# Down-weight sums dealt anew over the units of a GeGLU kernel, and raw down weights fetched a unit ahead

## The chip, the cores and the metric

The kernel runs on one core of a Trainium2 chip. The metric is the device time of one execution in microseconds (us). A core has five engines with queues of their own: TensorE (PE) for matmuls, VectorE (DVE), ScalarE (ACT), GpSimd (POOL) and SyncE (SP), which here issues all DMA transfers. SBUF is the on-chip memory, PSUM the eight banks into which TensorE writes, HBM the memory outside.

## The reference

```
def reference(x, w_gate, w_up, w_down):
    g = jnp.einsum("bsd,df->bsf", x, w_gate)
    u = jnp.einsum("bsd,df->bsf", x, w_up)
    h = _gelu(g) * u
    return jnp.einsum("bsf,fd->bsd", h, w_down)
```

x is 1 x 2048 x 1024, w_gate and w_up are 1024 x 3584, w_down is 3584 x 1024, all bf16. `_gelu` is the tanh form.

## The kernel before, in words

**Arithmetic.** Each of the three products is made by a Strassen-like scheme on 2 x 2 blocks: seven block products in place of eight, bought with sums of blocks. Sums of weights are called s1 to s4 (and sa, a cast), sums of x are t1 to t4 (and tb), and partial results that more than one output needs are taken out of PSUM by ACT (`snap`, L124) as p1, u2 and p5. Products of raw blocks run in bf16, products of sums in f32r. Two passes (`ip` = 0, 1) cover 1024 rows each, in two halves `c` of 512.

**Units.** The 3584 columns of gate and up are 14 units of 256. In pass 0, unit 0 is done plainly, units 1 to 3 and 12, 13 by `unit` (L239), units 4 to 11 two at a time by `pair0` (L339), which applies the scheme a second time to one product of the pair and saves two partial results, p5, to HBM (`pd`) for pass 1, where `pair1` (L437) reads them back. Each unit leaves two row blocks of h = gelu(g) * u; VectorE makes the product (`times`, L107 in the profile, as is every VectorE operation of this kind), ACT the gelu (L199). After its units, each pass runs `down` (L616), which multiplies h by w_down: first raw bf16 products that need `raw` slices of w_down (`fetch12`, L581: fourteen of 256 KB), then the forms with the sums ("w,q" in the profile).

**Sums of w_down.** w_down has 14 blocks `j`, and each needs three sums m. They are made once, in pass 0, stored to HBM (`td`) and read in both passes. Two ways exist. `keep_part` (L504) lets ACT copy a raw part into a free PSUM bank and VectorE subtract (three ACT and three DVE operations per block). `keep_whole` (L520) uses three POOL operations:

```
        m = [slot([P, N], f32r, "m") for _ in range(3)]
        pool(m[0], ra[:, N:], ra[:, :N], SUB)
        pool(m[1], rb[:, N:], m[0], SUB)
        pool(m[2], rb[:, :N], m[1], SUB)
```

`JS` (L62) deals the blocks to the pairs: the first two of an entry are made by ACT and DVE, a third by POOL. `making` (L783) deals the rest to units 12 and 13. `fetch_wd` (L491) loads the raw blocks they need, two transfers of 256 KB for each block.

**Order.** The order on SP, DVE and POOL, on PE, and mostly on ACT, is that of the program text (`manual_schedule`); each engine works strictly in that order and waits by semaphores. Memory is dealt by pools: `kpool` has 52 slots of 2 KB per partition, handed round in the order of the program (`slot`); a new tile takes a slot only when all that used the old one is done. So a change in the number of tiles moves every later tile to another slot, and with it the wait that comes before the tile's first write. `wpool` has three buffers of 8 KB (weights of a unit, some big loads, the staging `st8` for h), and other pools have one buffer for a name or tag.

**Memory for h.** `hT` holds the first 14 row blocks in SBUF. While `forms` (sums of x for the pairs) and `saved` (the partial results of a pair) are in use, there is no room for the rest, so units 7 to 11 write to `st8`, go out to HBM (`hd`, `keep_home` L336) and come back once `forms` and `saved` are free (five transfers out, five back, in `prepare` of unit 12, L880).

**Hooks.** `unit` calls `aside(0)` behind its first product, `keep` for the sums of w_down, and `prepare` as `after_p5`, where the next unit's sums are issued to POOL; `turned` (units 2 and 3) makes sums of x. `pair0` calls `hooks` with "w" (load a unit's weights), "made" (store m), "out", "pd" and "fetch". `more` (L939) puts the last stores of m into `down`, and `todo` runs an agenda of loads by step.

Of the kernel before, what the change touches and what calls it, by code (L numbers as in the profile page):

```python
# [10 lines left out]
def kernel(  # L11
# [23 lines left out]
    nc = tc.nc  # L35
# [23 lines left out]
    NWARM = 7  # L59
    SLOTS = 52  # L60
    FIRST, LAST = 4, 11
    JS = {4: (0, 1, None), 6: (2, 3, 4), 8: (5, 6, 7), 10: (8, 9, None)}  # L62
    JB = [js[1] for js in JS.values()]
    LAG = 3
    BIG12 = (0, 2, 4)
# [13 lines left out]
    def new_x():  # L79
        return [xpool.tile([P, NKB, N], bf16, name=f"xT{c}") for c in range(2)]  # L80

    NA = 10
    hT = hpool.tile([P, NJ, 2, N], bf16, name="hT")
    forms = hpool.tile([P, NA, N], f32r, name="forms", tag="h1")
    saved = hpool.tile([P, NJ - NA, N], f32, name="saved", tag="h2")
    h1 = {}

    def h1_part(n):
        if n not in h1:
            shape = [P, (NA, NJ - NA)[n], 2, N]  # L90
            h1[n] = hpool.tile(shape, bf16, name=f"hT{n}", tag=("h1", "h2")[n])
        return h1[n]

    def h(kh, j, c):
        at = hT if kh == 0 else h1_part(j >= NA)
        return at[:, j - NA * (kh and j >= NA), c, :]
    wdn = w_down.rearrange("(kh j p) d -> p kh j d", kh=2, p=P)

    def slot(shape, dtype, name):
# [139 lines left out]
    def unit(u, banks, s, t, late, after_p5, aside, keep, ahead_of_p4, behind_p4, turned):  # L239
        GU = range(2)  # L240
        e, c, d = banks
        aside(-2)
        g, up = late() if late else (None, None)
        aside(-1)
        for i in GU:
            product(e[i], s["s2"][i], t["t2"], False)
        aside(0)
        keep(0, c)
        u2 = [snap(e[i], "u2") for i in GU]
        if late:  # L250
            g = gelu(g)
        c11 = g, up
        keep(1, c)
        keep(2, c)
        c = d
        for i in GU:
            product(c[i], s["s1"][i], t["t1"], True)
        p5 = [snap(c[i], "p5") for i in GU]
        after_p5()
        for i in GU:  # L260
            product(e[i], s["s3"][i], t["t3"], False)
        if turned:
            g, up = add(e, p5)
            times(2 * u + 1, 1, gelu(g), up)
            turned(banks[1])
        else:
            g, up = new(dve, e[0], p5[0], ADD, "sum", dtype=f32), banks[1][not late]
            dve(up, e[1], p5[1], ADD)
        if late:
            times(2 * u, 0, *c11)  # L270
        for i in GU:
            product(c[i], s["s4"][i], t["tb"], False)
        if not turned:
            times(2 * u + 1, 1, gelu(g), up)
        aside(1)
        g, up = add(c, u2)
        times(2 * u, 1, gelu(g), up)
        ahead_of_p4()
        for i in GU:
            product(e[i], s["sa"][i], t["t4"], False)  # L280
        behind_p4()
        if turned:
            dve(e[1], e[1], p5[1], SUB)
        times(2 * u + 1, 0, gelu(e[0]), e[1])
# [1 line left out]

    H = KH // 2
    T1, T2, T3, T4, TB = [[forms[:, 2 * n + i] for i in range(2)] for n in range(5)]
    A, B = [[saved[:, 2 * n + i] for i in range(2)] for n in range(2)]
    pd = dpool.tile([P, LAST - FIRST + 1, 2, N], f32, name="pd")  # L290
    hd = dpool.tile([P, LAST - NU // 2 + 1, 2, 2, N], bf16, name="hd")
    lo = hT[:, 10:14].rearrange("p j c n -> p (j c) n")

    def small_sums(s, q):
# [39 lines left out]
        times(fb, c, g, up)  # L334

    def keep_home(u):  # L336
        nc.sync.dma_start(out=hd[:, u - NU // 2], in_=away[u][:, u % 2])

    def pair0(a, roles, S, t, js, hooks):  # L339
        F, C, K, E = roles  # L340
# [1 line left out]
        sa, sb = S[a], S[b]  # L342
        q = {}
        t1 = t["t1"]

        sa.make(*[x for x in ("s1", "s2", "s3") if x not in sa])
        sb.make(*[x for x in ("s1", "s2") if x not in sb])
# [11 lines left out]
            times(fb, 0, gelu(e[0]), e[1])  # L359

        def keep(j, n, ps):
            if j is not None:
                keep_part(j, n, ps[n % 2])

        ja, jb, jp = js
        if jp is not None:
            keep_whole(jp)
        hooks("w", n)
        keep(ja, 0, K)
        full(F, sa["s2"], t["t2"])  # L370
        u2a = [snap(F[i], "u2", spare[2 + i]) for i in range(2)]
        part(E, [x[:, :H] for x in sa["s1"]], t1[:H], True, False)
        p1 = [snap(E[i], "p1", A[i]) for i in range(2)]
        full(C, sb["s2"], t["t2"])
# [1 line left out]
        keep(ja, 2, K)  # L376
        hooks("made", ja)
        part(E, [x[:, H:] for x in sa["s1"]], t1[H:], False)
        p5a = [snap(E[i], "p5", spare[i]) for i in range(2)]
        u2b = [snap(C[i], "u2") for i in range(2)]  # L380
        full(F, sa["s3"], t["t3"])
        g, up = add(F, p5a)
# [1 line left out]
        full(E, sa["s4"], t["tb"])  # L384
        g = gelu(g)
        times(2 * a + 1, 1, g, up)
        hooks("made", jp)
        part(K, q["r2"], T2, False)
        u2r = [snap(K[i], "u2", B[i]) for i in range(2)]
        full(F, sa["sa"], t["t4"])  # L390
# [15 lines left out]
            dve(B[i], E[i], u2r[i], ADD)  # L406
        hooks("pd", a)
        hooks("fetch", a)
        p5b = [snap(K[i], "p5", spare[i]) for i in range(2)]
        raw1(F, W(n))  # L410
        g, up = add(C, p5b)
        p1n = [snap(F[i], "p1") for i in range(2)]
# [76 lines left out]
    wraw, made = {}, {}  # L489

    def fetch_wd(js):  # L491
        big = None
        for j in js:
            if j < NJ - 2:
                wraw[j] = [slot([P, Dm], bf16, "raw") for _ in range(2)]
            else:
                if big is None:
                    big = wpool.tile([P, 4, Dm], bf16, name="w")
                n = 2 * (j - NJ + 2)
                wraw[j] = [big[:, n + kh] for kh in range(2)]  # L500
            for kh in range(2):
                nc.sync.dma_start(out=wraw[j][kh], in_=wdn[:, kh, j, :])

# [15 lines left out]

    def keep_whole(j):  # L520
        ra, rb = wraw[j]
        m = [slot([P, N], f32r, "m") for _ in range(3)]
        pool(m[0], ra[:, N:], ra[:, :N], SUB)
        pool(m[1], rb[:, N:], m[0], SUB)
        pool(m[2], rb[:, :N], m[1], SUB)
        made[j] = m

    def store_made(j):
        if isinstance(made[j], list):
# [56 lines left out]

    agenda = {}

    def at(step, what, j):
        agenda.setdefault(int(step), []).append((what, j))

    for n in range(NJ):
        at(max(-1, 2 * n - 8), fetch12, n)
    for j in range(NJ):
        at(AT12[j], load12, j)
        at(AT12S[j], make12, j)
# [183 lines left out]

    def making(u):  # L783
        if u == NU - 2:
            return [10]
        return [11, 12, 13] if u == NU - 1 else []

    E, K, C, F = odd, cc, dd, even
    spare = [flat(xT[1][:, 2 * m : 2 * m + 2]) for m in range(4)]
    S, p5 = {}, {}  # L790

    def W(u):
# [39 lines left out]
    for ip in range(NPASS):  # L832
        with tc.manual_schedule(engines={ENG.Activation}):
# [6 lines left out]
            for u in range(1 if ip == 0 else 0, NU):  # L840
                if upgraded(u):
                    if u % 2:
                        continue
                    if u == FIRST:
                        S = {u: s, u + 1: sums_s(W(u + 1), pool)}
                        if ip == 0:
                            st8 = wpool.tile([P, 2, 2, 2, N], bf16, name="w")
                            away.update({n: st8 for n in range(NU // 2, LAST + 1)})

                    def hooks(what, n):  # L850
                        if what == "w":
                            W(n)
                            if ip and n <= LAST:
                                fetch_p5(n)
                        if what == "out" and n in away:
                            keep_home(n)
                        if what == "pd":
                            j = 0 if n % 2 else 2
                            nc.sync.dma_start(out=pd[:, n - FIRST], in_=saved[:, j : j + 2])
                        if what == "made" and n is not None:  # L860
                            store_made(n)
                        if what == "fetch":
                            js = JS.get(n + 2, making(LAST + 1))
                            fetch_wd([j for j in js if j is not None])

                    roles = F, C, K, E
                    if ip == 0:
                        F, C, K, E = pair0(u, roles, S, t, JS[u], hooks)
                    else:
                        F, C, K, E = pair1(u, roles, S, t, hooks)  # L870
                    if u + 1 == LAST:
                        s = make_s(None, pool, S[u + 2])
                        nxt["s"] = S[u + 3]
                        if ip == 0:
                            away.clear()
                    continue
# [3 lines left out]
                def prepare():  # L880
# [2 lines left out]
                    if u + 1 < NU:  # L883
                        nxt["s"] = make_s(W(u + 1), pool, nxt.get("s"))
                    if ip == 0:
                        if len(js) == 1:
                            store_made(js[0])
                        for j in js[1:]:
                            keep_whole(j)
                        if u >= LAST:  # L890
                            fetch_wd(making(u + 1))
                        if u == NU - 2:
                            for n in range(NU // 2, LAST + 1):
                                j = 2 * n - NJ
                                nc.sync.dma_start(out=h1_part(0)[:, j : j + 2], in_=hd[:, n - NU // 2])
                        if u == FIRST - 2:
                            fetch_wd(JS[FIRST][:2])

# [6 lines left out]
                def aside(part):  # L905
                    if first and part < 0:
                        rest_of_0(part + 2)
                    if part == 0 and u + 2 < NU:
# [2 lines left out]
                            fetch_p5(u + 2)  # L911
                        if (ip, u) == (0, 1):
                            load_lo()
                    if part == 0 and "t4" not in t:
                        t.make("t4")

# [73 lines left out]
```

## Time and profile before

| | |
|---|---|
| median of 3 runs | 549.48 us (549.23 to 550.05) |
| the profiled execution | 549.2 us |
| its span, first to last instruction | 547.4 us |
| mean granted TensorE clock | 0.997 |
| TensorE busy | 536.6 us, 2393 matmuls |
| DVE, ACT, POOL busy | 362.2, 276.4, 272.1 us |
| HBM read, written | 81.26 MB, 22.02 MB |

The span begins with the first and ends with the last instruction of the profiled execution; 1.8 us of its time lie around it. In the lists of groups and in the timeline, a row names the engine, the line, what is written and what is read ("bank<-raw,hT": into a PSUM bank, from `raw` and `hT`), the number of instructions, and in brackets the idle time ahead of the row and what ended it. Times in the timeline count from the start of the span. All matmuls have L131, POOL's sums L110, VectorE's operations L107, ACT's gelu L199, ACT's copies out of PSUM L124, ACT's casts of raw parts into PSUM L513. Pass 0 ends its units at about 201 us, and `down` of pass 0 begins at about 204 us.

### The profile page before, as it was taken

How to read it: one execution, taken by the hardware profiler on the slowest of the kernel's cores; microseconds unless marked ns; L12 is line 12 of the kernel's file. 1: busy time of each engine (PE TensorE's matmuls, PEld its weight loads, DVE VectorE, ACT ScalarE, POOL GpSimd, SP SyncE). 2: the span in 40 equal slices, each digit the busy share in tenths (PEclk: the TensorE clock that was granted, in tenths of full speed). 3: DMA queues.
4: the chain of work that ended last, by engine and by line, in shares of the span. 5: the costliest groups of instructions: out<-in, count | busy, mean ns of one | idle time of the engine just before them, and what ended most of it. 6: DMA issues, size and time to landing. Idle time of an engine off the chain costs nothing.

```text
span 547.4 us, 7631 instructions
## 1 busy us (share of the span) xinstructions
PE 536.6 (98%) x2393; PEld 377.6 (69%) x2393; DVE 362.2 (66%) x556; ACT 276.4 (50%) x497; POOL 272.1 (50%) x253
## 2 busy tenths in 40 slices
PE   9999999999999979999999999999999999999997
PEld 5568586757577654488886868667677685478885
DVE  2988867576776879258687464585765839766730
ACT  2557676777685740015543556556666561114431
POOL 1079937989898750000005966668988940000000
PEclk9999999999999999999999999999999999999999
DMA  9797046477779499999995643332642239673751
GB/s 242 176 230 198 1 135 219 164 265 247 249 260 325 158 363 399 375 305 204 231 290 172 174 116 117 111 112 85 193 126 69 76 113 385 214 229 98 222 190 50
DMA packets 119560, 107.99 MB, mean 197 GB/s; under 512 B 22240, under 2 KB 98016, under 8 KB 119520
## 3 DMA queue, kind: packets, MB, share of 16 engines
q1 hardware_dynamic: 119520, 107.50, 64.8%
q8 instruction: 19, 0.31, 0.2%
q14 instruction: 21, 0.17, 0.1%
HBM read 81.26 MB, written 22.02 MB: 189 GB/s over the span
## 4 chain that ended last, share of the span: by engine, by line
PE 77%; DMA 9%; POOL 5%; DVE 4%; issue 2%; ACT 2%; POOLq 0%; DVEq 0%; SPq 0%; ACTq 0%
PE bank L131 76%; DMA raw<-in_w_down_dram 7%; POOL s L110 3%; POOL r L110 2%; DMA pd<-saved 1%; DVE bank L107 1%; DMA td<-m 1%; ACT g L199 1%; PE bank L753 1%; DVE sum L107 1%; PE bank L698 1%; DVE m L107 1%; DVE hT L107 1%; ACT bank L513 0%; DVE w L107 0%
## 5 line engine op out<-in xcount | busy, mean ns | idle before, releaser
L110 POOL TENSOR_TENSOR s<-w 128x512 fp32r<-128x512 bf16 x102 | 122.1, 1217 | 143.3 <-PE bank L131 111.3
L131 PE MATMUL bank<-t,s 128*128 128x512 f32 x552 | 132.4, 392 | 0.6 <-DVE m L107 0.3
L131 PEld LDWEIGHTS bank<-t,s 128*128 128x128 f32 x552 | 103.3, 188 | 24.0 <-DVE m L107 0.8
L131 PE MATMUL bank<-xT,w 128*128 128x512 bf16 (+1 forms) x504 | 110.5, 376 | 0.4 <-ACT forms L824 0.4
L131 PEld LDWEIGHTS <-w 128*128 128x128 bf16 x504 | 47.7, 98 | 58.9 <-issue 4.9
L199 ACT ACTIVATE g<-sum 128x512 f32<-128x512 f32 x81 | 51.4, 634 | 70.2 <-DVE sum L107 64.6
L124 ACT COPY p<-bank 128x512 f32<-128x512 f32 x92 | 51.7, 589 | 43.3 <-PE bank L131 42.8
L110 POOL TENSOR_TENSOR s<-s,w 128x512 fp32r<-128x512 f32 x50 | 58.9, 1197 | 5.0 <-PE bank L131 4.7
L107 DVE TENSOR_TENSOR sum<-bank,p 128x512 f32<-128x512 f32 x54 | 36.4, 687 | 35.7 <-PE bank L131 35.7
L131 PE MATMUL bank<-q 128*128 128x512 f32 x240 | 58.9, 389 | 0.0
L110 POOL TENSOR_TENSOR s<-w,s 128x512 fp32r<-128x512 bf16 x50 | 57.6, 1176 | 0.0
L107 DVE TENSOR_TENSOR hT<-g,bank 128x512 bf16<-128x512 f32 x68 | 46.2, 688 | 16.5 <-ACT g L199 10.1
L131 PE MATMUL bank<-t,sa 128*128 128x512 f32 x216 | 55.1, 397 | 0.0
L131 PE MATMUL bank<-tb,s 128*128 128x512 f32 x216 | 54.8, 395 | 0.0
L131 PEld LDWEIGHTS bank<-q 128*128 128x128 f32 x240 | 45.1, 188 | 9.3
L119 ACT CAST tb<-raw 128x512 fp32r<-128x512 bf16 x28 | 17.3, 626 | 64.5 <-DMA raw<-in_w_down_dram 28.1
L131 PE MATMUL bank<-raw,hT 128*128 128x512 bf16 x192 | 43.6, 390 | 3.6 <-DMA raw<-in_w_down_dram 3.6
L131 PEld LDWEIGHTS bank<-tb,s 128*128 128x128 f32 x216 | 40.2, 188 | 9.9 <-POOL s L110 1.1
L131 PEld LDWEIGHTS bank<-t,sa 128*128 128x128 f32 x216 | 40.6, 188 | 9.1
L124 ACT COPY u<-bank 128x512 f32<-128x512 f32 x54 | 30.5, 594 | 17.8 <-PE bank L131 17.8
L131 PEld LDWEIGHTS <-hT 128*128 128x128 bf16 x192 | 19.2, 100 | 27.8 <-issue 6.7
L119 ACT CAST sa<-w 128x512 fp32r<-128x512 bf16 x54 | 30.9, 621 | 0.1
(81 smaller groups left out, 640.4 us busy)
## 6 DMA issues: line engine op xcount, KB each, us to landing
raw<-in_w_down_dram SPq DMA_DIRECT2D x76, 256.0 KB, 5.2
q<-td SPq DMA_DIRECT2D x60, 256.0 KB, 5.3
w<-in_w_gate_dram SPq DMA_DIRECT2D x27, 512.0 KB, 4.1
w<-in_w_up_dram SPq DMA_DIRECT2D x27, 512.0 KB, 5.4
td<-m SPq DMA_DIRECT2D x24, 256.0 KB, 3.8
w<-td SPq DMA_DIRECT2D x6, 1024.0 KB, 10.0
td<-m SPq DMA_DIRECT2D x6, 768.0 KB, 6.4
pd<-saved SPq DMA_DIRECT2D x8, 512.0 KB, 6.0
```

Of the source, the lines that this page charges most:

```text
L107: nc.vector.tensor_tensor(out=out, in0=a, in1=b, op=op)
L110: nc.gpsimd.tensor_tensor(out=out, in0=a, in1=b, op=op)
L119: nc.scalar.copy(out=t, in_=src)
L124: nc.scalar.copy(out=t, in_=ps)
L131: nc.tensor.matmul(ps, lhsT=lhs, rhs=rhs, start=start, stop=stop, skip_group_check=True)
L199: nc.scalar.activation(g, src, ACT.Gelu_apprx_tanh)
L698: nc.tensor.transpose(tp[:, ko, :], xn[i][:, ko * P : (ko + 1) * P], ident)
L753: nc.tensor.matmul(bank[3][:, :cols], lhsT=warm[:, :P], rhs=warm[:, :cols], start=True, stop=True)
```

## The change

The blocks of sums are dealt anew. Each pair makes two, both by ACT and DVE (POOL's blocks 4 and 7 leave the pairs). Unit 12 makes block 8 and unit 13 block 9 by ACT and DVE; POOL makes blocks 10 to 13, twelve operations in place of six, and they are queued in unit 12's `prepare`, behind the sums of unit 13, rather than in unit 13's. Blocks 11 to 13 are written into buffers of `wpool`. The raws that unit 13's blocks need are fetched in unit 12's `aside(0)`, into slots. The first four raws of `down` are fetched in unit 13's `aside(0)`.

`hT` grows to 18 row blocks, so that only units 9 to 11 go out to HBM: three transfers out and three back, units 9 and 10 in pair 10's "fetch" hook, unit 11 in unit 12's `aside(0)`. The late part of h, `hL`, shares its memory with `forms` alone. `saved` is gone: its four tiles are now halves of `xT[1]`, and the copies of u2 and p5 that stood there take slots, six more per pair. In unit 3 `turned` stands ahead of `add(e, p5)`, whose three VectorE operations move behind `add(c, u2)`.

```diff
-    JS = {4: (0, 1, None), 6: (2, 3, 4), 8: (5, 6, 7), 10: (8, 9, None)}
+    JS = {4: (0, 1), 6: (2, 3), 8: (4, 5), 10: (6, 7)}
...
-    NA = 10
-    hT = hpool.tile([P, NJ, 2, N], bf16, name="hT")
-    forms = hpool.tile([P, NA, N], f32r, name="forms", tag="h1")
-    saved = hpool.tile([P, NJ - NA, N], f32, name="saved", tag="h2")
...
+    NH = NJ + 4
+    hT = hpool.tile([P, NH, 2, N], bf16, name="hT")
+    forms = hpool.tile([P, NFB - NH, N], f32r, name="forms", tag="h")
+    h1 = []
+
+    def late_h():
+        if not h1:
+            h1.append(hpool.tile([P, NFB - NH, 2, N], bf16, name="hL", tag="h"))
+        return h1[0]
...
-        if turned:
+        if turned and u % 2:
+            turned(banks[1])
+        elif turned:
             g, up = add(e, p5)
             times(2 * u + 1, 1, gelu(g), up)
             turned(banks[1])
...
         g, up = add(c, u2)
         times(2 * u, 1, gelu(g), up)
+        if turned and u % 2:
+            g, up = add(e, p5)
+            times(2 * u + 1, 1, gelu(g), up)
...
-    A, B = [[saved[:, 2 * n + i] for i in range(2)] for n in range(2)]
...
+    AWAY = NH // 2
+    hd = dpool.tile([P, LAST - AWAY + 1, 2, 2, N], bf16, name="hd")
...
+    def take_back(u):
+        j = 2 * u - NH
+        nc.sync.dma_start(out=late_h()[:, j : j + 2], in_=hd[:, u - AWAY])
...
+        A, B = [[flat(xT[1][:, 2 * m : 2 * m + 2]) for m in (2 * n, 2 * n + 1)] for n in range(2)]
...
-        ja, jb, jp = js
-        if jp is not None:
-            keep_whole(jp)
+        ja, jb = js
...
-        u2a = [snap(F[i], "u2", spare[2 + i]) for i in range(2)]
+        u2a = [snap(F[i], "u2") for i in range(2)]
...
-        p5a = [snap(E[i], "p5", spare[i]) for i in range(2)]
+        p5a = [snap(E[i], "p5") for i in range(2)]
...
-        hooks("made", jp)
...
-        p5b = [snap(K[i], "p5", spare[i]) for i in range(2)]
+        p5b = [snap(K[i], "p5") for i in range(2)]
...
         for j in js:
-            if j < NJ - 2:
-                wraw[j] = [slot([P, Dm], bf16, "raw") for _ in range(2)]
-            else:
...
+            wraw[j] = [slot([P, Dm], bf16, "raw") for _ in range(2)]
...
-        m = [slot([P, N], f32r, "m") for _ in range(3)]
+        if j < NJ - 3:
+            m = made[j] = [slot([P, N], f32r, "m") for _ in range(3)]
+        else:
+            made[j] = wpool.tile([P, 4, N], f32r, name="w")
+            m = [made[j][:, n] for n in range(3)]
...
     for n in range(NJ):
-        at(max(-1, 2 * n - 8), fetch12, n)
+        at(max(-1, 2 * n - 8), need12, n)
...
         if u == NU - 2:
-            return [10]
-        return [11, 12, 13] if u == NU - 1 else []
+            return [8]
+        return [9, 10, 11, 12, 13] if u == NU - 1 else []
...
                         if what == "fetch":
-                            js = JS.get(n + 2, making(LAST + 1))
-                            fetch_wd([j for j in js if j is not None])
+                            fetch_wd(JS.get(n + 2, making(LAST + 1)))
+                            if n + 1 == LAST:
+                                for m in range(AWAY, LAST):
+                                    take_back(m)
...
                     if ip == 0:
-                        if len(js) == 1:
+                        if js:
                             store_made(js[0])
-                        for j in js[1:]:
-                            keep_whole(j)
-                        if u >= LAST:
-                            fetch_wd(making(u + 1))
                         if u == NU - 2:
-                            for n in range(NU // 2, LAST + 1):
-                                j = 2 * n - NJ
-                                nc.sync.dma_start(out=h1_part(0)[:, j : j + 2], in_=hd[:, n - NU // 2])
+                            for j in making(u + 1)[1:]:
+                                keep_whole(j)
+                        if u == NU - 1:
+                            store_made(js[1])
...
+                    if part == 0 and (ip, u) == (0, NU - 2):
+                        fetch_wd(making(u + 1))
+                        take_back(LAST)
+                    if part == 0 and (ip, u) == (0, NU - 1):
+                        for n in range(4):
+                            fetch12(n)
+                            ahead12.add(n)
```

`need12` calls `fetch12` unless the raw is in `ahead12` already.

More of the change, by code (lines that the diff above doesn't have):

```diff
@@ L80, in new_x @@
         return [xpool.tile([P, NKB, N], bf16, name=f"xT{c}") for c in range(2)]
-    NA = 10
-    hT = hpool.tile([P, NJ, 2, N], bf16, name="hT")
-    forms = hpool.tile([P, NA, N], f32r, name="forms", tag="h1")
-    saved = hpool.tile([P, NJ - NA, N], f32, name="saved", tag="h2")
[L86 to L92, printed above, removed]
+    NH = NJ + 4
[6 more added lines that the diff above has]
+        return h1[0]
     def h(kh, j, c):
-        at = hT if kh == 0 else h1_part(j >= NA)
-        return at[:, j - NA * (kh and j >= NA), c, :]
+        fb = kh * NJ + j
+        return hT[:, fb, c, :] if fb < NH else late_h()[:, fb - NH, c, :]
     wdn = w_down.rearrange("(kh j p) d -> p kh j d", kh=2, p=P)
@@ L288 @@
     T1, T2, T3, T4, TB = [[forms[:, 2 * n + i] for i in range(2)] for n in range(5)]
-    A, B = [[saved[:, 2 * n + i] for i in range(2)] for n in range(2)]
     pd = dpool.tile([P, LAST - FIRST + 1, 2, N], f32, name="pd")
-    hd = dpool.tile([P, LAST - NU // 2 + 1, 2, 2, N], bf16, name="hd")
+    AWAY = NH // 2
+    hd = dpool.tile([P, LAST - AWAY + 1, 2, 2, N], bf16, name="hd")
     lo = hT[:, 10:14].rearrange("p j c n -> p (j c) n")
@@ L336, in keep_home @@
     def keep_home(u):
-        nc.sync.dma_start(out=hd[:, u - NU // 2], in_=away[u][:, u % 2])
+        nc.sync.dma_start(out=hd[:, u - AWAY], in_=away[u][:, u % 2])
+    def take_back(u):
+        j = 2 * u - NH
+        nc.sync.dma_start(out=late_h()[:, j : j + 2], in_=hd[:, u - AWAY])
     def pair0(a, roles, S, t, js, hooks):
@@ L361, in keep @@
         def keep(j, n, ps):
-            if j is not None:
-                keep_part(j, n, ps[n % 2])
-        ja, jb, jp = js
-        if jp is not None:
-            keep_whole(jp)
+            keep_part(j, n, ps[n % 2])
+        ja, jb = js
         hooks("w", n)
@@ L491, in fetch_wd @@
     def fetch_wd(js):
-        big = None
         for j in js:
-            if j < NJ - 2:
-                wraw[j] = [slot([P, Dm], bf16, "raw") for _ in range(2)]
-            else:
[L497 to L500, printed above, removed]
+            wraw[j] = [slot([P, Dm], bf16, "raw") for _ in range(2)]
             for kh in range(2):
@@ L525, in keep_whole @@
         pool(m[2], rb[:, :N], m[1], SUB)
-        made[j] = m
     def store_made(j):
@@ L585, in fetch12, with need12 @@
         raw[1, n] = rl
+    ahead12 = set()
+    def need12(n):
+        if n in ahead12:
+            ahead12.remove(n)
+        else:
+            fetch12(n)
     agenda = {}
@@ L784, in making @@
         if u == NU - 2:
-            return [10]
-        return [11, 12, 13] if u == NU - 1 else []
+            return [8]
+        return [9, 10, 11, 12, 13] if u == NU - 1 else []
     E, K, C, F = odd, cc, dd, even
-    spare = [flat(xT[1][:, 2 * m : 2 * m + 2]) for m in range(4)]
     S, p5 = {}, {}
@@ L847 @@
                             st8 = wpool.tile([P, 2, 2, 2, N], bf16, name="w")
-                            away.update({n: st8 for n in range(NU // 2, LAST + 1)})
+                            away.update({n: st8 for n in range(AWAY, LAST + 1)})
                     def hooks(what, n):
@@ L857, in hooks @@
                         if what == "pd":
-                            j = 0 if n % 2 else 2
-                            nc.sync.dma_start(out=pd[:, n - FIRST], in_=saved[:, j : j + 2])
-                        if what == "made" and n is not None:
+                            k = 0 if n % 2 else KH
+                            nc.sync.dma_start(
+                                out=pd[:, n - FIRST].rearrange("p i n -> p (i n)"),
+                                in_=flat(xT[1][:, k : k + KH]),
+                            )
+                        if what == "made":
                             store_made(n)
                         if what == "fetch":
-                            js = JS.get(n + 2, making(LAST + 1))
-                            fetch_wd([j for j in js if j is not None])
+                            fetch_wd(JS.get(n + 2, making(LAST + 1)))
+                            if n + 1 == LAST:
+                                for m in range(AWAY, LAST):
+                                    take_back(m)
                     roles = F, C, K, E
@@ L913, in aside @@
                             load_lo()
+                    if part == 0 and (ip, u) == (0, NU - 2):
[3 more added lines that the diff above has]
+                        for n in range(4):
+                            fetch12(n)
+                            ahead12.add(n)
                     if part == 0 and "t4" not in t:
```

## The prediction

> **What bounds the kernel now.** I read the page's busy shares and its chain first, then TensorE's waits, then the timeline and the table of windows around the places that the change touches.
>
> ```profile
> PE 536.6 (98%) x2393; PEld 377.6 (69%) x2393; DVE 362.2 (66%) x556; ACT 276.4 (50%) x497; POOL 272.1 (50%) x253
> ...
> PE 77%; DMA 9%; POOL 5%; DVE 4%; issue 2%; ACT 2%; POOLq 0%; DVEq 0%; SPq 0%; ACTq 0%
> ```
>
> TensorE is busy 98% of the span of 547.4 us. The matmuls stay the same in kind and number (2393) under the change, so it can only move TensorE's idle time and its clock. The waits of TensorE by releaser:
>
> ```profile
> PE bank L131 <- DMA raw<-in_w_down_dram: 4.3, 4, 3.3
> ...
> PE bank L131 <- ACT saved L124: 0.4, 2, 0.2
> PE bank L131 <- DVE w L107: 0.4, 1, 0.4
> PE bank L131 <- DVE hT L107: 0.4, 1, 0.4
> PE bank L131 <- ACT forms L824: 0.4, 1, 0.4
> PE bank L131 <- DVE m L107: 0.3, 1, 0.3
> PE bank L131 <- ACT u L124: 0.2, 1, 0.2
> ```
>
> The columns are the total, the count and the longest wait. One wait stands out: 3.3 us at the start of `down`, when unit 13 is done and the first raw down weights are still on their way. The timeline of TensorE and the windows there:
>
> ```profile
> 198.96 1.98 PE L131 MATMUL bank<-t,sa 128*128 128x512 f32 x8
> 204.25 19.11 PE L131 MATMUL bank<-raw,hT 128*128 128x512 bf16 x80 [3.31 <-DMA raw<-in_w_down_dram]
> ...
> 231.36 0.81 PE L131 MATMUL bank<-w,q 128*128 128x512 f32 x2
> ```
>
> ```profile
> 200.00:210.00 10.00, 6.69 (x24) 2.82 (x23) 9.64 (x15) 1.12 (x2) 2.36 (x3) 0.83 1.02 364
> 210.00:220.00 10.00, 10.00 (x48) 4.55 (x47) 9.64 (x16) 2.05 (x4) 0.00 (x0) 1.00 1.06 398
> ```
>
> The columns end with the granted clock, the DMA share and GB/s. After the idle stretch the clock is 0.83 over ten microseconds: half clock for some 3.4 us, which costs 1.7. The DMA engines are full, at 364 to 398 GB/s. So this border costs 3.31 + 1.7, and 0.96 of later waits on raws (0.30, 0.44 and 0.22 in the same timeline).
>
> **The change, part by part.**
>
> *Raws of `down` a unit ahead.* The first four raws (256 KB each) are issued in unit 13 rather than behind it, and unit 13's ten are issued in unit 12 rather than behind unit 13's sums. Five transfers of h (the trips of units 7 and 8, out and back) go. So 3.31 + 1.7 us go at the border, if TensorE gets there when it did.
>
> *Unit 3.* Its `turned` now runs ahead of `add(e, p5)`, so ACT's copies into `forms` (58.82 and 59.54) no longer stand behind three VectorE operations. TensorE's wait at 59.46 goes: −0.4, and −0.6 with the gap around it.
>
> *Pairs 6 and 8.* POOL loses `keep_whole` (three operations) in each, but it was idle for 10.97 us there before its sums, so nothing is gained by that. The pool of 52 slots is dealt anew: the gelu that waited for `r4` now takes the slot that s4's first operation frees, about 0.7 later (106.86 becomes 107.54), while the second gelu's wait shrinks as POOL runs one operation earlier. Net +0.3 each, +0.6 for both. The `u2` copies now take slots that td stores must release first; with the other transfers gone those land in time. If not, 2.4 to 3.8 us per pair, by the landing times of before.
>
> *Pair 10.* No stall before. Its gelu now waits for s4's first operation (167.28 in before, 1.1 earlier with the shorter POOL chain, so 166.2) instead of running at 163.79; gelu 0.63 and VectorE's product 0.69 follow, and the second half of r1's product waits until 167.6 rather than 166.25: +1.35.
>
> *Unit 12.* The late h no longer shares memory with `saved`, so VectorE's wait for the pd transfer goes:
>
> ```profile
> 176.91 0.69 DVE L107 TENSOR_TENSOR hTTrue<-g,bank 128x512 bf16<-128x512 f32 x1 [1.54 <-DMA pd<-saved]
> ```
>
> With it go TensorE's stalls at 183.25 (0.33) and 185.61 (0.24) with their small followers, 1.4 in all. So unit 13 starts where it did, at 191.3: −0.6 + 0.6 + 1.35 − 1.4 = −0.05.
>
> *Unit 13, the new wait.* POOL made blocks 12 and 13 (six operations) within unit 13, where it was idle. Now it makes 10 to 13, twelve operations, right behind unit 13's sums:
>
> ```profile
> 186.19 2.32 POOL L110 TENSOR_TENSOR s<-w,s 128x512 fp32r<-128x512 bf16 x2
> 195.23 1.17 POOL L110 TENSOR_TENSOR m<-w 128x512 fp32r<-128x512 bf16 x1 [6.72 <-PE bank L131]
> 196.48 2.44 POOL L110 TENSOR_TENSOR m<-w,m 128x512 fp32r<-128x512 bf16 x2
> ```
>
> One block is 1.17 + 2.44 with its gap, 3.69 us. The sums themselves took 179.46 to 188.51, 9.05 us; but the first now takes a slot that VectorE's sum of unit 12 frees at 183.7 (it ran at 183.11 for 0.68). So the sums end at 183.7 + 9.05 = 192.75, and the blocks at 196.45, 200.15, 203.85 and 207.5. As the waits of the changed program stand, ACT's results in unit 13 get slots that these operations read last:
>
> ```profile
> 190.94 0.63 ACT L199 ACTIVATE g<-sum 128x512 f32<-128x512 f32 x1 [1.41 <-DVE sum L107]
> 191.47 0.58 ACT L199 ACTIVATE g<-bank 128x512 f32<-128x512 f32 x1
> 193.79 0.59 ACT L513 CAST bank<-raw 128x512 f32<-128x512 bf16 x1 [1.74 <-DMA raw<-in_w_down_dram]
> 194.32 1.07 ACT L124 COPY u<-bank 128x512 f32<-128x512 f32 x2
> ```
>
> The gelu at 191.47 waits for block 10 (196.45). Behind it on ACT stand the cast and the `u2` copies that free TensorE's banks: 196.45 + 0.6 + 0.55 + 0.6 = 198.2, and TensorE, due there at 194.9, idles 3.3 us. The second `u2` copy waits for block 11 (200.15, + 0.6 = 200.75): TensorE is due at 199.1, 1.65 more. The `p5` copies come 0.65 late once more. Unit 13's last eight matmuls follow: it ends at 200.94 + 3.3 + 1.65 + 0.65 − 0.4 (small gaps that are absorbed) = **206.1**, 5.2 later. A td store stands on the sums' path too, part two of pair 10's block: it lands at 185.04 in before and about 184.9 here, just in time. Bounds: nothing, if the slots come free earlier, and +8, if the sums slip three microseconds.
>
> The 3.3 us of idle is as long as the one that was followed by half clock, so half clock is likely from 198.2. For 3.4 us it covers eight matmuls, whose 1.8 extra the 1.65 and 0.65 waits hide: 0 to 0.5, I take 0.1. The Trainium skill (TensorE: Matmul & The Clock Gate, "Part 1: The HAM clock gate") says that a free-running window of about 3.4 us decides, and that a mostly idle one halves the clock; by that rule the broken stretch of 198 to 206 may hold the clock down longer. Before's trace shows one such drop only (0.83 above), and it ended after one window; the rival below has the price.
>
> *Start of `down`.* Raws 0 to 3 have landed (the fetch of the second waits for block 11's first operation, 198). TensorE starts at 206.1, on full clock. Only later raws can be waited for. In before the stretch took 231.36 − 204.25 = 27.1 us, of which 1.7 are the clock and 0.96 the waits, so 24.45 without them (112 matmuls at 0.216 are 24.2). Raws 4, 5 and 6 stand on SP behind the stores of blocks 11, 12 and 13, which POOL ends at 200.15, 203.85 and 207.5. From 207.5 SP may issue all the rest: 0.79 MB of store, eight raws (2.1), three `w` loads of 1.05 and two `q` (0.5), 6.5 MB, at 375 GB/s (between the windows' 364 and 398) 17.4 us, plus some 2 to land: 227, where raw 13 is needed at 228.6. I take 0.3 of waits, with bounds of 0 and 1.5. The w,q stage starts at 206.1 + 24.45 + 0.3 = 230.85, where before had 231.36: **−0.5**. The Trainium skill (DMA: Bandwidth & Descriptors, "Bandwidth") gives about 358 GB/s as what HBM allows one core; by that figure the raws would come about 0.8 later. The trace moved 398 in a window, so it disagrees and I go by the trace.
>
> From there on the program's order is the same, and I found no new wait in pass 1.
>
> **Sum.** −0.5 on the profiled run (549.2), so 548.7; the median of the three runs, 549.48, stands 0.28 above it: **549.0**. About 0.2% (1.1 us) is the least that a measurement of this kernel can tell from no change. So the 5.0 us won at the border are paid again inside unit 13.
>
> **Rivals.**
> 1. *The wait in unit 13 is shorter* (faster). For it: POOL is 50% busy, and VectorE's sum at 183.11 stood behind the pd wait of 1.54, which goes; against: TensorE is later by then. If POOL starts at 182.2, unit 13 ends 1.5 earlier: 547.5. If the slots do not bite at all, unit 13 ends at 200.9, and the raws become the bound: raw 13 lands at 227 where it is needed at 223.4, so the w,q stage comes at 200.9 + 24.45 + 3.6 = 228.95, which is 2.4 ahead of before: 547.1; with the stores earlier too, by up to 1.5, 545.6. Chance 0.32.
> 2. *The clock stays at half through the broken rest of unit 13* (slower). Place: the 24 matmuls from 198.2 on, 5.45 us at full clock; the price is 5.45 less the 2.3 of waits that hide it, +3.1: 552.1. It decides if the windows after the stall count as idle. Pulling the same way, at +2.4 to +3.8, is a td store that a `u2` copy of pair 8 or 10 must await. For it: the 0.83; against: there it lasted one window. Chance 0.30.
> 3. *No net change* (the forecast): 548.4 to 550.6, chance 0.38. That the early raws do not come early, because their fetch waits for POOL's slots, is part of it: it needs the second raw after 206, where I have 200.
>
> Range for 8 in 10: 545.8 to 552.4. Faster 0.32, within 0.2% 0.38, slower 0.30.
>
> **What would show it.** Right: TensorE's largest waits lie in unit 13, on ACT's `u` copy, about 3.3 and 1.65, with ACT waiting for POOL's m; no wait on raw at the start of `down`; POOL busy without a break from 184 to 207; VectorE's pd wait and the stall on `forms` gone. Wrong: ACT in unit 13 never waits for POOL (rival 1), a granted clock well under 0.83 in 198 to 208 (rival 2), or waits on td stores in pairs 6 to 10.

## The result, and the profile after

The changed kernel takes 553.23 us (median of 4 runs, 552.33 to 553.29) against 549.36 (4 runs, 548.38 to 550.05): the ratio is 1.0068, with a 95% interval of 1.0049 to 1.0087. It is slower by 3.9 us, 0.8 us above the top of the forecast range. The profiled span is 551.4 us.

First the waits of TensorE, in the columns shown above for before (total, count, longest):

```profile
PE bank L129 <- ACT u L122: 4.5, 2, 3.9
PE bank L129 <- DVE hT L105: 2.7, 3, 1.2
PE bank L129 <- DMA raw<-in_w_down_dram: 2.1, 3, 1.4
```

The wait at the start of `down` is gone, and a longer one has taken its place on ACT's u copies, which is where the prediction put it. The waits on `hT` (0.4 in before) lie in unit 3 and in pairs 6 and 8; the net cost of those places is in the list near the end. The timeline of TensorE around unit 13 and `down`:

```profile
191.75 3.79 PE L129 MATMUL bank<-t,s 128*128 128x512 f32 x16
199.46 1.95 PE L129 MATMUL bank<-t,s 128*128 128x512 f32 x4 [3.92 <-ACT u L122]
201.96 2.07 PE L129 MATMUL bank<-t,s 128*128 128x512 f32 x4 [0.55 <-ACT u L122]
203.83 3.19 PE L129 MATMUL bank<-tb,s 128*128 128x512 f32 x8
206.86 2.02 PE L129 MATMUL bank<-t,sa 128*128 128x512 f32 x8
208.72 15.93 PE L129 MATMUL bank<-raw,hT 128*128 128x512 bf16 x72
...
227.79 3.61 PE L129 MATMUL bank<-raw,hL 128*128 128x512 bf16 x16 [1.41 <-DMA raw<-in_w_down_dram]
```

The same number of matmuls takes longer after the stop: eight of them take 3.19 us at 203.83, and 2.06 in before (at 197.06). The table of windows says why; its last three columns are the granted clock, the DMA share and GB/s:

```profile
195.00:200.00 5.00, 1.08 (x5) 0.59 (x4) 1.98 (x3) 2.23 (x4) 4.76 (x5) 0.96 0.47 186
200.00:205.00 5.00, 4.45 (x11) 3.01 (x10) 2.47 (x4) 3.05 (x6) 4.76 (x6) 0.50 0.52 176
205.00:210.00 5.00, 5.00 (x20) 3.30 (x20) 3.81 (x7) 1.41 (x3) 3.37 (x3) 0.86 1.04 393
```

The clock is at half for (0.04 + 0.50 + 0.14) x 5 x 2 = 6.8 us, twice as long as in before, and from 195 to 205 us the DMA engines run at half load. ACT's timeline shows what held the u copies, with one releaser to distrust:

```profile
195.24 0.63 ACT L197 ACTIVATE g<-sum 128x512 f32<-128x512 f32 x1 [5.32 <-DMA hL<-hd]
197.71 0.60 ACT L197 ACTIVATE g<-bank 128x512 f32<-128x512 f32 x1 [1.84 <-POOL m L108]
198.21 0.59 ACT L510 CAST bank<-raw 128x512 f32<-128x512 bf16 x1
198.72 0.59 ACT L122 COPY u<-bank 128x512 f32<-128x512 f32 x1
201.32 0.59 ACT L122 COPY u<-bank 128x512 f32<-128x512 f32 x1 [2.01 <-POOL w L108]
```

```profile
194.02 1.19 POOL L108 TENSOR_TENSOR m<-raw 128x512 fp32r<-128x512 bf16 x1
195.28 2.40 POOL L108 TENSOR_TENSOR m<-raw,m 128x512 fp32r<-128x512 bf16 x2
...
198.87 2.41 POOL L108 TENSOR_TENSOR w<-raw,w 128x512 fp32r<-128x512 bf16 x2
```

The gelu at 195.24 has nothing to do with the load of late h that is named beside it: it begins 0.03 us after the end of POOL's first operation of block 10 (194.02 + 1.19 = 195.21), which read the slot that it takes. The next begins when the third operation ends (195.28 + 2.40 = 197.68), and the second u copy, at 201.32, when block 11 ends (198.87 + 2.41 = 201.28).

Both profiles have the same 2393 matmuls in the same order, so their starts can be subtracted one by one. After minus before: +0.4 us where unit 13 starts, +7.9 where it ends, +2.8 once `down` is at full clock, +4.1 from raw 10 (counted from 0) on to the end. So the balance is 0.4 (up to unit 12) + 7.5 (unit 13) − 5.1 (the border) + 1.3 (later raws) = 4.1.

### The profile page after: what moved, and what is told of

Same layout as the page of the kernel before. It is cut to its first block, busy times and chain, and to the rows that moved or that the text cites. A ratio compares the mean times of both kernels' runs of the same rounds, so it can differ in the third digit from the quotient of the medians.

```text
span 551.4 us, 7602 instructions
## 1 busy us (share of the span) xinstructions
PE 536.5 (97%) x2393; PEld 378.7 (69%) x2393; DVE 361.9 (66%) x556; ACT 276.8 (50%) x497; POOL 270.8 (49%) x253
## 4 chain that ended last, share of the span: by engine, by line
PE 57%; DVE 2%; DMA 2%; issue 0%; ACT 0%; SPq 0%
PE bank L129 57%; DVE q L105 2%; DMA raw<-in_w_down_dram 2%; ACT st L671 0%; SPq L550 0%; SPq L584 0%
## 5 line engine op out<-in xcount | busy, mean ns | idle before, releaser
L108 POOL TENSOR_TENSOR s<-w 128x512 fp32r<-128x512 bf16 x102 | 120.8, 1206 | 155.9 <-PE bank L129 120.6
L129 PE MATMUL bank<-t,s 128*128 128x512 f32 x552 | 134.4, 396 | 5.0 <-ACT u L122 4.5
L122 ACT COPY p<-bank 128x512 f32<-128x512 f32 x108 | 60.5, 591 | 46.7 <-PE bank L129 46.3
L105 DVE TENSOR_TENSOR sum<-bank,p 128x512 f32<-128x512 f32 x62 | 41.9, 687 | 38.5 <-PE bank L129 37.6
L129 PEld LDWEIGHTS bank<-tb,s 128*128 128x128 f32 x216 | 41.4, 192 | 9.5 <-issue 0.5
L122 ACT COPY u<-bank 128x512 f32<-128x512 f32 x62 | 35.4, 594 | 21.8 <-PE bank L129 18.9
L105 DVE TENSOR_TENSOR bank<-bank,p 128x512 f32<-128x512 f32 x56 | 39.0, 696 | 5.3 <-PE bank L129 4.9
L129 PE MATMUL bank<-raw,hT 128*128 128x512 bf16 x144 | 31.6, 379 | 0.1
```

The lines of the kernel that those rows point to most:

```text
L105: nc.vector.tensor_tensor(out=out, in0=a, in1=b, op=op)
L108: nc.gpsimd.tensor_tensor(out=out, in0=a, in1=b, op=op)
L122: nc.scalar.copy(out=t, in_=ps)
L129: nc.tensor.matmul(ps, lhsT=lhs, rhs=rhs, start=start, stop=stop, skip_group_check=True)
```

## The experiments

All ratios are to the kernel before, run beside them on the same chip.

**e3: the same queues, other slots.** In the changed kernel, the calls that make blocks 10 to 13 on POOL are written in unit 13's `prepare`. POOL has nothing else between, so no engine's order changes; only the slots are dealt otherwise.

```diff
-                        if u == NU - 2:
-                            for j in making(u + 1)[1:]:
+                        if u == NU - 1:
+                            for j in js[1:]:
                                 keep_whole(j)
-                        if u == NU - 1:
                             store_made(js[1])
```

> The changed kernel with one edit: POOL's twelve operations for blocks 10 to 13 are written in unit 13's prepare and not in unit 12's. POOL's own order, SP's, VectorE's, ACT's and TensorE's stay the same; only the dealing of the slots changes, since the raws and sums of blocks 10 to 13 now take and give back slots later in the program's order. Theory (slots): ACT no longer waits for POOL in unit 13, TensorE's 4.5 us of waits on ACT's u copy and the two windows of half clock (7.9 us against before at the end of unit 13) go; down starts near 201.5; later raws stand behind the store of block 13, which POOL ends at 208.5, and cost 3 to 4 us; 547.5 us in all, between 546 and 548.5. Rival (the load of late h, which the profile names as what ended ACT's wait of 5.3 us): unchanged, 553. Rival (POOL's twelve operations are simply late, whoever waits): 551 to 553.

Measured: 550.29 us, ratio 1.002 (1.0005 to 1.0035). The waits on the u copies are gone, but another stands two steps later. TensorE and VectorE of e3:

```profile
200.87 3.39 PE L129 MATMUL bank<-tb,s 128*128 128x512 f32 x8 [3.68 <-ACT p L122]
```

```profile
198.38 0.69 DVE L105 TENSOR_TENSOR m<-bank,raw 128x512 fp32r<-128x512 f32 x1 [5.31 <-issue]
```

The load of late h, the same in both, is ruled out as the cause. The slots are shown to be it for the first wait, and the time fell short of my 547.5 because of a second wait: VectorE's first m of block 9 writes into the single tile of `mpool`, which block 8's store reads. The profile has no name for this wait ("issue"), but that store, which stands behind ten raws on the DMA queue, landed at 198.30, 0.08 us before the row above. In the changed kernel it landed at 197.8, hidden behind the wait on POOL. The half clock here lasts 3.4 us: the granted clock is 0.66 in 200 to 205 and 1.00 on both sides.

**e4: two results out of the slots.** The last two gelus of unit 12 go into a free half of `xT[1]`.

> The changed kernel with the last two gelus of unit 12 written into a free half of xT[1] and not into slots, so that the u2 copies of unit 13 take the slots that come free two steps earlier, and one p5 copy and a gelu wait for block 11. Theory (slots, and a clock that drops only after a long idle stretch): the first wait of unit 13 (3.9 us) goes, one of about 4 us appears at the second p5 copy (block 11 at 201.3, due at 197.5), then no more; if that idle stretch is long enough half clock follows it, for the last 12 matmuls: unit 13 ends 4 to 6 us after before's, and the total is 551 to 552.5. If the wait falls on the end of the unit and the clock stays full: 549 to 550.5. Rival (h's load): 553.

Measured: 550.20 us, ratio 1.0014 (1.0000 to 1.0028). TensorE of e4:

```profile
199.98 3.51 PE L129 MATMUL bank<-tb,s 128*128 128x512 f32 x8 [3.13 <-ACT p L122]
```

The first wait went as expected, so two ways of avoiding the slots agree (e3 is 550.29). But the wait that followed (3.13 us) is that of e3, the store of block 8, which landed at 197.4, 0.1 us before VectorE's first m of block 9; it is not block 11, and the total came out below the 551 to 552.5 that I gave for a clock that drops.

**e7: the second wait too.** e3, with block 9's sums in `xT[1]`:

```diff
+        elif part == 0 and j == 9:
+            made[j] = [flat(xT[1][:, 2 * n : 2 * n + 2]).bitcast(f32r) for n in range(3)]
         elif part == 0:
             made[j] = mpool.tile([P, 3, N], f32r, name="m")
...
```

> The edit of e3, and the sums m of block 9 in a free half of xT[1] and not in the single tile of mpool, which block 8's store must leave first (it landed at 198.3 in e3, and VectorE's first m of block 9 began at 198.38). Theory (a second wait lay behind the one on POOL's slots: that store, queued behind ten raws): TensorE's wait of 3.7 us on ACT's p copies in unit 13 goes, and the half clock behind it; unit 13 ends at 201.3 and down starts there; but the DMA engines then are the bound, as in e1, and the waits on raws grow from 2.0 to 4 us or so: 547.5 to 548.5 us. Rival (the p copies wait for POOL or for the raws of block 9): 550.

Measured: 550.26 us, ratio 1.0024 (1.0008 to 1.0040), as e3. Unit 13 now runs without a stop, and `down` starts at 200.42. Yet nothing is gained; TensorE of e7:

```profile
200.42 8.81 PE L129 MATMUL bank<-raw,hT 128*128 128x512 bf16 x40
209.81 1.89 PE L129 MATMUL bank<-raw,hT 128*128 128x512 bf16 x8 [0.59 <-DMA raw<-in_w_down_dram]
215.14 7.03 PE L129 MATMUL bank<-raw,hT 128*128 128x512 bf16 x24 [3.44 <-DMA raw<-in_w_down_dram]
```

All that was won is waited for again, 3.44 us at once on raw 6, with half clock behind it (0.66 in 215 to 220). The second wait was real, and its price was nothing, since the raws were the next bound. I expected that bound and sized it too low (5.4 us of waits on raws, where I had 4). It is not the bytes alone: the DMA share is 0.74 from 205 to 210 us and 0.88 from 210 to 215. SP issued raw 6 only at 210.37, behind block 13's store, and POOL had ended that block at 209.92.

**e9: the second wait alone.** The changed kernel with block 9's sums in `xT[1]`, POOL's calls where they were.

> The changed kernel with block 9's sums in xT[1] alone (POOL's operations stay in unit 12's prepare). Theory (ACT's waits on POOL's slots end later than block 8's store, 198.8 against 197.8): nothing gained, 553 us, within 0.7 of the changed kernel. Rival (the store is the cause, the slots are not): 549 to 550.

Measured: 551.84 us, ratio 1.0055 (1.0038 to 1.0071): 1.4 below the changed kernel, where I expected nothing; the two intervals overlap, so the size is uncertain. Unit 13 is as it was (3.92 us on the u copy). The profile has the gain in the raws, whose waits fall from 2.1 to 0.9:

```profile
PE bank L129 <- DMA raw<-in_w_down_dram: 0.9, 3, 0.5
```

The likely reason is that block 9's store is now three stores, of which the first can leave when its own part is made, and SP stands still for less long (DMA share 0.84 in 200 to 205 against 0.52).

**e5: the store that holds SP.** In the changed kernel, the stores of blocks 9 and 10 moved from unit 13 to step 19 of `down` (both; the expectation below says 19 and 20), behind the last raw. SP of the changed kernel (the second column is how long a group of issues took):

```profile
190.72 9.51 SPq L584 DMA_DIRECT2D raw<-in_w_down_dram  x4
203.94 0.34 SPq L533 DMA_DIRECT2D td<-m  x1
...
206.96 0.58 SPq L533 DMA_DIRECT2D td<-w  x1
```

> The changed kernel with the stores of blocks 9 and 10 moved from unit 13 to steps 19 and 20 of down, behind the last raw on SP's queue; nothing else. Theory (the raws of down were late because SP stood at the store of block 9 until VectorE had made it at 203.9, with the DMA engines at half load from 195 to 205 us): unit 13 stays as it is, 7.9 us late at its end, the 2.1 us of waits on raws go: 551.2 us. Rival (the raws are late because POOL makes blocks 11 to 13 late): 553, as the changed kernel.

Measured: 550.18 us, ratio 1.0011 (1.0000 to 1.0022), 3 below the changed kernel and so a microsecond better than expected. Unit 13 still waits 5.0 us on the u copies, and no wait on raws is left at all. So the late raws were due to these two stores. In the changed kernel SP stood from 200.2 to 203.9 at block 9's store until VectorE had made it, behind the stalled ACT; block 11's store, ready at 201.3, and raw 4 were behind it. In e5 the DMA share is 0.99 from 200 to 205, against 0.52. The edit also takes the 1.57 MB of the two stores out from ahead of the raws, and e5 alone does not tell the two apart; e9, which leaves the bytes where they are, takes away 1.2 of the 2.1 us.

**e6 and e8: the other stores.** e6 is e3 with the stores of blocks 12 and 13 moved to steps 4 and 8; e8 is e7 with that, and with the stores of blocks 9 and 10 behind the last raw.

> The edit of e3, and the stores of blocks 12 and 13 moved on SP's queue from steps 0 and 2 of down to steps 4 and 8, so that raws 5 to 8 no longer stand behind POOL's end of those blocks. Theory (the raws' lateness in down is SP's order, on top of the bytes): waits on raws fall from 3 to 4 us (e3) to 1 to 2: 545.5 us, 2 below e3. If the bytes alone set it: equal to e3 within 0.5.

> The edits of e7, and the stores of blocks 9 and 10 (1.57 MB) moved behind the last raw of down on SP's queue, those of blocks 12 and 13 to steps 4 and 8. Theory (with nothing to wait for in unit 13, the bytes ahead of the last raw set when the w,q stage starts): the raws land up to 4 us earlier than in e7, so 544 to 545 us. Rival (TensorE is bound by something else in unit 13 or after the raws): equal to e7.

Measured: e6 549.88 (1.0007; 0.9994 to 1.0020), equal to e3; e8 548.42 (0.9989; 0.9978 to 1.0000), 1.8 below e7, where I expected up to 4 from the raws. In e6, SP still stood at block 9's store until 201. In e8 it stands at block 11's store, which POOL ends at 201.33, with raw 4 behind it; the windows of e8:

```profile
195.00:200.00 5.00, 5.00 (x24) 4.14 (x23) 4.45 (x7) 2.42 (x5) 4.77 (x5) 1.00 0.86 314
200.00:205.00 5.00, 5.00 (x24) 2.37 (x24) 4.64 (x6) 0.67 (x2) 4.76 (x5) 1.00 0.57 165
```

TensorE never stops in these ten microseconds, but the DMA engines are idle for 2.9 of them, and 4.7 us of waits on raws come later.

**e1: is it the order or the bytes?** Now the kernel before, with the first four raws issued ahead of the five loads of h:

```diff
...
                         if u == NU - 2:
+                            for n in range(4):
+                                fetch12(n)
+                                ahead12.add(n)
                             for n in range(NU // 2, LAST + 1):
...
```

> The kernel before, with one part alone: the first four raws of down are issued in unit 12's prepare, ahead of the five loads of h (hd) that stand before them on SP's queue; nothing else moves. Theory A (the border is a matter of the queue's order): the wait of 3.3 us at the start of down goes, with the half clock behind it (1.7), and about 1 us of it comes back as waits on later raws: about 545.5 us, 4 below before. Theory B (the DMA engines are full from 190 to 230 us, so that the bytes set when the last raw lands): the wait at the border goes, but the same time is spent waiting for raws 8 to 13, and the w,q stage starts where it did: 549 us, within 0.7 of before.

Measured: 549.72 us, ratio 1.0005 (0.9991 to 1.0018). The wait of 3.3 us and the half clock are gone in the profile, and the kernel is no faster. Waits of TensorE in e1, then one of its windows:

```profile
PE bank L131 <- DMA raw<-in_w_down_dram: 4.6, 7, 1.0
```

```profile
205.00:210.00 5.00, 3.98 (x19) 1.76 (x18) 4.90 (x8) 0.00 (x0) 0.00 (x0) 1.00 1.03 406
```

The one long wait has become seven short ones with a larger sum, at a DMA share of 1.02 to 1.07 from 195 to 230 us. Theory B holds: the w,q stage starts at 230.81 (231.36 in before), and with the DMA engines full it is the bytes ahead of the last raw that set this. The next two runs move those bytes and the time from which they flow.

**e10 and e12: fewer bytes ahead, and an earlier start.** e10 is e1 with the stores of blocks 11 to 13 at steps 19 to 21, behind the last raw; e12 is e10 with the raw blocks of unit 13 fetched in unit 12's `aside(0)`, as the change has it. In the kernel before these are six transfers (three blocks), not the ten that the expectation names; ten is the number in the changed kernel.

```diff
...
-            if step in (-1, 0, 2):
-                store_made({-1: NJ - 3, 0: NJ - 2, 2: NJ - 1}[step])
+            if step in (19, 20, 21):
+                store_made(step - 19 + NJ - 3)
...
```

> The kernel before with the edit of e1 (four raws ahead of the loads of h), and the stores of blocks 11 to 13 (2.36 MB) moved from steps -1, 0 and 2 of down to steps 19 to 21, behind the last raw. Theory (bytes): 2.36 MB at 385 GB/s are 6.1 us; the 4.6 us of waits on raws in e1 go, and with them what before loses at the border: 545 us. Rival (the waits only move to the q loads behind): 548 to 549.

> The edits of e10 on the kernel before, and one more part of the change: the ten raws for unit 13 are fetched in unit 12's aside(0), which lets the DMA engines (load 0.39 from 185 to 190 us in e10) begin some 3 us earlier. Theory (bytes): what e10 has left of waits on raws and q loads, 0.8 and 1.0, goes: 544 us. Rival (block 10's store now stands behind the raws and holds VectorE's block 11 in unit 13, as in e3): 546 to 548.

Measured: e10 545.22 us, ratio 0.9930 (0.9910 to 0.9951); e12 542.16 us, ratio 0.9874 (0.9860 to 0.9889), 7.7 below the 549.86 beside it and more than I expected. In e10 the DMA engines are still at 0.39 from 185 to 190 us; in e12 they work there, and TensorE does not wait for a raw at all:

```profile
185.00:190.00 5.00, 5.00 (x22) 3.89 (x22) 3.83 (x8) 3.73 (x8) 3.59 (x4) 1.00 0.99 354
```

```profile
199.80 20.89 PE L131 MATMUL bank<-raw,hT 128*128 128x512 bf16 x94
220.53 3.62 PE L131 MATMUL bank<-raw,hTTrue 128*128 128x512 bf16 x15
223.80 8.54 PE L131 MATMUL bank<-w,q 128*128 128x512 f32 x36
```

The w,q stage starts at 223.80, where before had 231.36. (Some matmul records are missing from this trace: 94 and 15 stand for 96 and 16.) e12 is the fastest kernel of this study. What it takes from the change is the early raws alone; the late stores are not part of the change.

## Why the prediction was wrong

The place and the mechanism of the main cost were right. The total and its sign were not: −0.5 was forecast and +4.1 came, and of the 4.6 between them unit 13 has 2.3, the later raws 2.0 and the start of unit 13 the rest.

- *Unit 3, pairs, unit 12*: forecast −0.05 at the start of unit 13, measured +0.4. Unit 3's gain is −0.1 rather than −0.6, since moving `add(e, p5)` back costs 0.47 at 63.5; another −0.2 stood already at 7 us, ahead of all that the change touches. Pairs 6 and 8 cost 0.2 each (forecast 0.3), pair 10 1.5 (1.35); 1.1 came back behind it rather than 1.4. Of the feared waits on td stores by a `u2` copy one came, in pair 10: ACT waited 0.70 at 157.05 and TensorE 0.51 behind it. It cost nothing, because the gelu at 166.23 waits for POOL anyway, which works without a break from 154 to 167.
- *Unit 13, the new wait*: the mechanism was right, as e3 and e4 show, and the size off: +7.5 against 5.2. Two terms were mis-sized. POOL's sums began at 184.32 and not 183.7, and stopped 0.65 us for the td store that I had "just in time"; they ended at 194.0 rather than 192.75, so the idle time was 3.92 and not 3.3. The later waits came to 0.55 rather than 1.65 + 0.65 − 0.4, as the matmuls between them ran at half clock. And the half clock, taken at 0.1 because those waits would hide it, held for 6.8 us: with 3.92 + 0.55 of waits, some 3.0 of the 7.5 are the clock. This is rival 2, which I gave 0.30 and priced at 3.1. By the Trainium skill's page TensorE: Matmul & The Clock Gate ("Part 1: The HAM clock gate"), the clock is decided per window of about 3.4 us. The runs agree with that length: before after 3.31 us idle, e3 after 3.68, e4 after 3.13, e6 after 3.14 and e7 after 3.44 show one such window; the changed kernel, e5 and e9, each after 3.92, show two. The three with two are those in which TensorE stops once more, on the second u copy, while the clock is at half (0.55, 1.10 and 0.45 us). No run changes that second stop alone, so that it is the cause is read from the traces (last section) and not tested.
- *The border*: −5.1 measured, −5.0 forecast. It came because unit 13 ended so late that the first raws had landed; in e7, where unit 13 does not stop, it is paid again as waits on raws.
- *Later raws*: this step failed. I put raw 4 behind block 11's store (200.15) and overlooked block 9's, which stands ahead of both on SP and waits for VectorE behind the stalled ACT: 2.1 us of waits in place of 0.3, and +1.3 against before where the forecast has −0.7. e5 takes the waits away, and 3 us in all.
- *What the reasoning lacked as a whole*: I counted 5 us as the border's price because its wait and its half clock came to that. e1 shows that price to be nothing by itself: the DMA engines were full until 230 us, and TensorE waited for raws instead. My own rival 1 said that the raws become the bound once unit 13 does not wait, and gave 547.1; e7 is that case, with 550.3. The rival looked at raw 13 alone; what bound first was raw 6 behind block 13's store, a wait of 3.44 us with half clock behind it. A second wait (block 8's store) that I did not see lay behind the first, and cost nothing in the end, since the raws were the next bound.

What stays open is how much the shorter trips of h and the larger `hT` are worth alone; no run here has them without the new deal of the sums.

## What to carry to other kernels

A wait for a transfer is worth its length only if the transfer engines had time to spare: look at the DMA share from the moment the transfers could have begun until the last one is needed, and if it is full there, move bytes out of that stretch (stores that nobody needs yet) or start it earlier; the place in the queue alone gave nothing here (e1). Where a pool deals its memory in the order of the program, queueing slow work early on an idle engine ties its slots to that work's end, and a fast engine that comes later pays; the same queue order with the calls written later avoids it. And for each engine that issues transfers in order, list all that stand ahead and what each of them waits for, not only the slowest one.

## What the runs showed of the hardware

In the twelve profiles, up to the last matmul, the granted clock changes only after whole multiples of 3.413 us: in the changed kernel it is full for 57 such stretches, at half for two (199.55 to 206.38), then full for 101. On that grid the share of a stretch in which TensorE was busy goes with what the clock does next.

- At full clock, the stretches followed by half clock were busy for 0.36 of their time or less (the changed kernel 0.03, before 0.06, e7 0.36). Those busy for 0.55 or more (the least in e7 and e8) were not followed by it.
- At half clock, the clock stayed there after a busy share of 0.84 (the changed kernel, with its stop of 0.55 us), 0.75 (e9) and 0.68 (e5). It came back after 0.91 (e4) and 1.00 (the other runs).

So stops of 1.50 and 1.03 us left the clock full in e8, while one of 0.55 us behind a long stop goes with a second stretch at half clock, 3.4 us at half speed or about 1.7 us lost. The ends of matmuls are modelled, so the shares are rough, and between these limits no run tells. The second stretch is no accident of one execution: the mean granted clock is 0.993 or 0.994 in all 18 executions of the changed kernel, e5 and e9. In the kernel before it goes from 0.994 to 1.000, so there the half clock is not the same in every execution.

Full DMA engines moved 381 GB/s over 30 us in before (200 to 230) and 388 to 392 in e10, e1 and e12 (195 to 225). Over 5 us, at a DMA share of 1.00 to 1.07, it was anything from 316 (e8, 185 to 190) to 411 (e7, 200 to 205). So a term worked out from bytes is good to a few per cent over 30 us, and not over 5.
